# Moving two row sums and a transposing DMA in a fused attention and SwiGLU kernel

## The chip, the cores and the metric

The kernel runs on one core of a Trainium2 chip. The metric is the device time of one execution in microseconds: the median of three runs of the kernel before is 557.85 us (557.7 to 557.88). A profile is one further execution, with every instruction recorded. Engines: TensorE (PE) multiplies matrices into PSUM banks, VectorE (DVE), ScalarE (ACT) and GpSimd (POOL) work on tiles, SyncE (SP) issues DMAs. Each engine takes its instructions strictly in the order in which the program gives them, and waits on semaphores where one depends on another engine.

## The reference

Two stages follow each other. First an attention with projected keys and values (8 batches, 8 heads, 1024 tokens, head dimension 64, 64 projected keys):

```python
k_proj = np.einsum('ks,bhsd->bhkd', E, k)
v_proj = np.einsum('ks,bhsd->bhkd', F, v)
scores = scale * np.matmul(q, k_proj.transpose(0, 1, 3, 2))
attn = np.exp(scores - np.max(scores, axis=-1, keepdims=True))
attn = attn / (np.sum(attn, axis=-1, keepdims=True) + 1e-09)
attn_out = np.matmul(attn, v_proj)
```

Then a gated feed-forward block over the 8192 tokens of 512 features, with 1536 hidden features:

```python
g = x @ w_gate
silu = g * (1.0 / (1.0 + np.exp(-g)))
out = (silu * (x @ w_val)) @ w_out
```

Inputs and output are float32 in HBM.

## The kernel before

**Chunks and iterations.** The feed-forward work is cut into 16 chunks of 512 tokens, two per batch, and each chunk into 12 iterations f, one per 128 hidden features. The main loop (L986 to L995) runs over these 192 iterations. In each, f_g (L534) multiplies four gate matmuls into a gps bank, ScalarE takes the Silu, f_v (L544) multiplies four value matmuls into a vps bank, and VectorE multiplies the two into hT (L550). There are two gps and two vps banks.

**The output product.** w_out is applied with a seven-product scheme of quarter blocks: h_sum (L600) adds or subtracts quarters of hT, w_sum does so for w_out, and f_m (L676) runs the products of the chunk *before*, in 14 steps: seven (n = 0 to 6) for the first half of the tokens, seven for the second, each of six matmuls (m_mm, L624). After some steps come combinations: m_34 (L648; a ScalarE copy and a GpSimd add) after n = 1, m_52 (L655) after n = 3, m_16 (L660; a VectorE add at L663, then a GpSimd subtraction at L664) after n = 5, m_7 (L666; a VectorE add at L669 and the output DMA on SP) after n = 6. The seventh product, n = 6, is accumulated into the bank that m_16's add has read, so it follows that add. Step n runs at f = (0, 1, 2, 3, 4, 4, 5) for the first half and (6, 7, 8, 9, 10, 10, 11) for the second (L981). The sums for m = 1, 6 and 7 are each one wide VectorE instruction at the ends of f = 1, 2, 3 of the next chunk (L980); those for m = 5 and 2 go to GpSimd in small pieces at f = 6 to 11 (L972).

**Slots.** While the chunks of batch b - 1 run, the attention of batch b is prepared. Its steps are written into a table of slots by hand (put, L732; place, L735). An iteration t has two slots: 2t between f_g and f_v, and 2t + 1 behind f_v and behind all late work of the iteration (h_sum and f_m). A batch b has a stretch of 48 slots beginning at s0 = 48 (b - 1): slots 0 to 23 lie in the first chunk of the stretch (A below), 24 to 47 in the second (B). All slot numbers below are relative to s0. So in chunk B, slot 26 is before hT of f = 1, slot 28 before hT of f = 2, 30 before hT of f = 3; slot 33 is behind m_16 of the first half, slot 35 behind its m_7.

**The steps of attention.** A batch has eight score units j of 128 by 512 scores. For each, u_S (L357) multiplies q by the projected keys and ScalarE takes the exponential into a tile ee; u_R (L393) takes row sums and reciprocals on VectorE (L397, L398); u_N (L401) normalises on GpSimd (L412) into a tile AAd and calls u_Z (L426), which adds the row sums into a check sum zsum on GpSimd (L428). Units 0 to 3 belong to the first half of the batch's tokens, 4 to 7 to the second. When four units are normalised, u_AD (L349) issues a transposing DMA on SP, from AAd into a tile AT. u_PVt multiplies AT by the projected values much later: for the second half at slot 56. There are four ee tiles, two AAd tiles and two AT tiles.

**Other entries of the slots.** u_TD (L341) issues the transposing DMA of q on SP: for the next batch at slots 42 and 44. The loads of k, v and two q halves of the batch after are issued by GpSimd at slots 24, 26, 28 and 30 of the stretch (batch 2's stretch: 28, 30, 32 and 34; batch 7's has none); within a slot loads go first (L960). In batch 7's stretch slot 38 also holds u_sum (L772), which reduces zsum on VectorE, and slot 40 a small matmul that reads its result.

Before the change the units of the second group have their scores at slots 25, 25, 27, 27, their row sums and normalisations at 26, 27, 30, 31, and their transposing DMA at 36.

Of the kernel before, what the change touches and what calls it, by code (L numbers as in the profile page):

```python
# [42 lines left out]
def kernel(  # L43
# [688 lines left out]
    def put(s, fn, *a):  # L732
        slots[s].append((fn, a))

    def place(b):  # L735
        s0 = 48 * (b - 1)
        if b == 1:
            put(22, u_TD, 1, 0)
            put(29, u_K1, 1)
            put(32, u_KT, 1)  # L740
            put(40, u_V1, 1)
            sa = (35, 36, 37, 38, 41, 42, 43, 44)
            put(41, u_AD, 1, 0)
            put(30, u_TD, 1, 1)
            put(47, u_AD, 1, 1)
            put(46, u_PVt, 1, 0, (0, 1), ("aa", "av"))
        else:
            if b == 2:
                put(s0 + 10, u_KV, b)
            else:  # L750
                put(s0 + 8, u_KV, b, "kv", (0, H), "v")
            put(s0 + (13 if b == 2 else 11), u_KT, b)
            put(s0 + (9 if b == 2 else -6), u_TD, b, 0)
            put(s0 + (11 if b == 2 else -4), u_TD, b, 1)
            sa = [s0 + j for j in ((15, 15, 17, 17) if b == 2 else (13, 13, 15, 15)) + (25, 25, 27, 27)]
            put(s0 + 25, u_AD, b, 0)
            put(s0 + 36, u_AD, b, 1)
            put(s0 + 44, u_PVt, b, 0, (0, 1), ("aa", "yz"))
        for j in range(NJ):
            put(sa[j], u_S, b, j)  # L760
            at = sa[j] + (1 if b == 1 else 1 + j % 4)
            put(at, u_R, b, j)
            put(at, u_N, b, j)
        put(s0 + (68 if b == 1 else 56), u_PVt, b, 1, (0, 1), ("aa", "yz"))
# [52 lines left out]
    with tc.manual_schedule():  # L817
# [132 lines left out]
        for b in range(1, B):  # L950
            place(b)
        for b in range(2, B):
            s0 = 48 * (b - 1) - (20 if b == 3 else 24)
            at = (43, 43, 44, 45) if b == 2 else (s0, s0 + 2, s0 + 4, s0 + 6)
# [75 lines left out]
```

## Time and profile before

| what | us |
|---|---|
| median of 3 runs | 557.85 |
| the profiled execution, time | 558.25 |
| the profiled execution, span from first to last instruction | 556.6 |
| TensorE busy | 538.9 |
| VectorE busy | 323.7 |
| GpSimd busy | 308.0 |
| ScalarE busy | 262.1 |

The time of the profiled execution lies 1.65 us over its span. Busy time is the sum over an engine's instructions, averaged over the whole run; it doesn't tell what one stretch is bound by. A row of the timeline reads: start in us, duration in us, engine, line, operation, output<-input, shapes, count, and in square brackets the idle time of the engine before it with what ended that. Where several matmuls are merged, the duration is that of the group; the ends of matmuls are modelled, so the distance of two starts is the safer measure. A row of the list of waits reads: engine, waiting line, what it waited for, total us, times, longest.

### The profile page before, as it was taken

To read this page: it belongs to the slowest core of one execution; us is meant where nothing else is said; L and a number is where in the kernel's file an instruction comes from. 1 tells how busy PE (TensorE), PEld (TensorE's weight loads), DVE (VectorE), ACT (ScalarE), POOL (GpSimd) and SP (SyncE) were. 2 spreads that over 40 slices of the span, in tenths; PEclk is the share of its full clock that TensorE was granted. 3 is DMA by queue.
4 is the path that set the end of the run, shared out by engine and by line. 5 is a ranking of instruction groups with operands and counts; after the bars stand their busy time and mean duration, and the time that the engine had idled before them with its cause. 6 is when DMAs were issued, how large, how long until landed. Compare 5 with 4: busy or idle time off the path is not lost. (4 is left out here: it accounts for less than half of the span.)

```text
span 556.6 us, 9399 instructions
## 1 busy us (share of the span) xinstructions
PE 538.9 (97%) x3558; PEld 314.2 (56%) x3558; DVE 323.7 (58%) x546; ACT 262.1 (47%) x441; POOL 308.0 (55%) x428
## 2 busy tenths in 40 slices
PE   7999999998999989999999989999899999999996
PEld 4654545565556655556455555566555665555565
DVE  3787884667356654568346483465835666343553
ACT  3565453672446624556336544465344652442321
POOL 6862494468517764197532974248660666425162
PEclk9999999999999999999999999999999999999999
DMA  9999969728941894109910299114990023010003
GB/s 200 189 197 190 181 134 182 159 75 127 205 86 39 161 217 114 39 1 208 234 51 38 61 181 214 39 39 87 199 179 30 38 77 77 38 39 38 7 33 118
DMA packets 112226, 62.92 MB, mean 113 GB/s; under 512 B 65968, under 2 KB 103856, under 8 KB 112176
## 3 DMA queue, kind: packets, MB, share of 16 engines
q0 software_dynamic: 43952, 29.49, 37.2%
q1 hardware_dynamic: 67392, 31.46, 23.3%
q10 hardware_dynamic: 832, 1.31, 0.8%
q8 instruction: 29, 0.48, 0.3%
q14 instruction: 21, 0.17, 0.1%
HBM read 60.29 MB, written 16.78 MB: 138 GB/s over the span
## 5 line engine op out<-in xcount | busy, mean ns | idle before, releaser
L525 PE MATMUL vps<-xT,wv 128*128 128x512 bf16 (+1 forms) x776 | 197.6, 377 | 0.9 <-DMA wv<-in_moe_w_val_dram 0.9
L525 PE MATMUL gps<-xT,wg 128*128 128x512 bf16 (+1 forms) x772 | 196.5, 377 | 0.0
L550 DVE TENSOR_TENSOR hT<-th,vps 128x512 bf16<-128x512 f32 x156 | 106.3, 682 | 143.6 <-PE vps L525 130.1
L541 ACT ACTIVATE th<-gps 128x512 f32<-128x512 f32 x156 | 93.2, 597 | 185.1 <-PE gps L525 180.6
L617 POOL TENSOR_TENSOR hs<-hT 128x256 bf16<-128x256 bf16 x180 | 118.4, 683 | 50.4 <-DVE hT L550 47.9
L525 PEld LDWEIGHTS <-wv 128*128 128x128 bf16 x776 | 74.1, 98 | 91.0 <-issue 6.5
L634 PEld LDWEIGHTS <-hs 128*128 128x128 bf16 x900 | 88.0, 98 | 43.7 <-issue 9.6
L525 PEld LDWEIGHTS <-wg 128*128 128x128 bf16 x776 | 74.1, 98 | 51.4 <-issue 0.2
L664 POOL TENSOR_TENSOR tt<-tt,ysb 128x512 f32<-128x512 f32 x28 | 35.5, 1268 | 89.6 <-DVE tt L663 89.5
L412 POOL TENSOR_TENSOR AAd<-ee,zr 128x512 bf16<-128x512 f32 x56 | 58.5, 1044 | 47.8 <-ACT ee L375 17.6
L634 PE MATMUL yps<-ws,hs 128*128 128x256 bf16 x540 | 68.6, 273 | 8.2 <-DVE tt L663 8.1
L617 DVE TENSOR_TENSOR hs<-hT 128x1536 bf16<-128x1536 bf16 (+1 forms) x49 | 57.9, 1187 | 0.1
L397 DVE TENSOR_REDUCE zr<-ee 128x8 f32<-128x512 f32 x64 | 43.3, 677 | 20.5 <-ACT ee L375 20.2
L634 PE MATMUL yps<-ws,hT 128*128 128x256 bf16 x360 | 48.8, 273 | 0.0
L634 PE MATMUL yps<-wo,hs 128*128 128x256 bf16 x360 | 48.6, 273 | 0.1
L653 POOL TENSOR_TENSOR tt<-xs 128x256 f32<-128x256 f32 x30 | 22.8, 761 | 40.3 <-ACT xs L651 40.3
L634 PEld LDWEIGHTS <-hT 128*128 128x128 bf16 x360 | 35.2, 98 | 16.0
L375 ACT ACTIVATE ee<-sc 128x512 f32<-128x512 f32 x64 | 35.7, 606 | 4.3 <-PE sc L367 2.9
L658 ACT COPY ysb<-yps 128x512 f32<-128x512 f32 x30 | 17.6, 586 | 27.3 <-PE yps L634 27.3
L651 ACT COPY xs<-yps 128x512 f32<-128x512 f32 x30 | 17.7, 590 | 25.1 <-PE yps L634 25.0
L480 ACT CAST xT<-pv 128x512 bf16<-128x512 f32 x56 | 28.7, 599 | 0.0
L538 ACT ACTIVATE th<-gps 128x512 f32<-128x512 f32 x35 | 20.9, 598 | 16.5 <-PE gps L525 16.5
(112 smaller groups left out, 407.9 us busy)
## 6 DMA issues: line engine op xcount, KB each, us to landing
out_dram<-ysb SPq DMA_DIRECT2D x27, 512.0 KB, 2.9
qb<-in_q_dram POOLq DMA_DIRECT2D x14, 512.0 KB, 13.1
kb<-in_k_dram POOLq DMA_DIRECT2D x7, 1024.0 KB, 10.9
vb<-in_v_dram POOLq DMA_DIRECT2D x7, 1024.0 KB, 15.2
wo<-in_moe_w_out_dram POOLq DMA_DIRECT2D x2, 768.0 KB, 21.8
out_dram<-ysb SPq DMA_DIRECT2D x6, 256.0 KB, 2.4
kraw<-in_k_dram ACTq DMA_DIRECT2D x2, 512.0 KB, 4.9
qb<-in_q_dram POOLq DMA_DIRECT2D x4, 256.0 KB, 7.9
```

The lines of the kernel that those rows point to most:

```text
L375: nc.scalar.activation(out=e[:].rearrange("p h j k -> p (h j k)"), in_=ps[:].rearrange("p a k -> p (a k)"), func=AF.Exp, scale=scale,)
L397: nc.vector.reduce_sum(out=z, in_=e[:], axis=AX.X)
L412: eng.tensor_tensor(out=a.rearrange("p j h k -> p h j k"), in0=ee.pop((b, u))[:], in1=r.unsqueeze(3).to_broadcast([P, 4, 2, KP]), op=ALU.mult,
L480: nc.scalar.copy(out=xT[b, ch][:, kt, :], in_=ps[:])
L525: nc.tensor.matmul(out=ps[:, ts], lhsT=(wg, wv)[w][:, kt, f * P : (f + 1) * P], rhs=x[:, kt, ts], start=(kt == 0), stop=(kt == NKT - 1),)
L538: nc.scalar.activation(out=th[:], in_=ps[:], func=AF.Tanh, scale=0.5)
L541: nc.scalar.activation(out=th[:], in_=ps[:], func=AF.Silu)
L550: nc.vector.tensor_tensor(out=hT[c][:, f, :], in0=th[:], in1=ps[:], op=ALU.mult)
L617: eng.tensor_tensor(out=hs[c, m][:, fs, :], in0=quarter(hT[c], *a)[:, fs], in1=quarter(hT[c], *b)[:, fs], op=op,)
L634: nc.tensor.matmul(out=ps, lhsT=lhsT, rhs=ws[m][:, f, :] if rhs is None else rhs, start=(start and f == 0), stop=(f == HF - 1), skip_group ...
L653: nc.gpsimd.tensor_tensor(out=t[:, 0], in0=xs[:, 0], in1=xs[:, 1], op=ALU.add)
L664: nc.gpsimd.tensor_tensor(out=t[:], in0=t[:], in1=yo[c, p][:, 1:3], op=ALU.subtract)
```

## The change

For batches 2 to 7 the row sums and the normalisations (with their additions to zsum) of units 4 to 7 are put at slots 26, 28, 33 and 35 instead of 26, 27, 30 and 31. The transposing DMA of the second group is put at slot 38 instead of 36. Units 0 to 3 stay at their slots (the expression for them is the former one), and so does all of batch 1.

```diff
             put(s0 + 25, u_AD, b, 0)
-            put(s0 + 36, u_AD, b, 1)
+            put(s0 + 38, u_AD, b, 1)
             put(s0 + 44, u_PVt, b, 0, (0, 1), ("aa", "yz"))
         for j in range(NJ):
             put(sa[j], u_S, b, j)
-            at = sa[j] + (1 if b == 1 else 1 + j % 4)
+            at = sa[j] + 1 if b == 1 else sa[j] + 1 + j % 4 if j < 4 else s0 + (26, 28, 33, 35)[j - 4]
             put(at, u_R, b, j)
             put(at, u_N, b, j)
```

## The prediction

> **What bounds the kernel now.** I read three views in turn: the page for the engine that is always busy, the list of waits for what ever stops it, and the timeline around one stop. Unit names as in the section on the kernel: sum1, sum6, sum7 are the three whole-width h_sum calls on VectorE (L617), q0 and q1 the two q loads that GpSimd issues, A and B the two chunks of a batch's stretch.
>
> ```profile
> PE 538.9 (97%) x3558; PEld 314.2 (56%) x3558; DVE 323.7 (58%) x546; ACT 262.1 (47%) x441; POOL 308.0 (55%) x428
> L634 PE MATMUL yps<-ws,hs 128*128 128x256 bf16 x540 | 68.6, 273 | 8.2 <-DVE tt L663 8.1
> PE yps L634 <- DVE tt L663: 8.1, 6, 1.5
> ```
>
> TensorE is busy 538.9 of 556.6 us. Of its few waits one stands out: product 7 waits for the add of m_16 (L663), 8.1 us in six waits. Taken window by window, it falls once in the stretch of each of batches 2 to 7: five of 1.5 us and, for batch 7, one of 0.6. They sit always at f = 5 of chunk B, where product 7 of the first half (f_m n = 6) overwrites the bank that m_16 must have read. The fifth of them on VectorE, GpSimd and TensorE:
>
> ```profile
> 391.58 1.04 POOL L412 TENSOR_TENSOR AAd<-ee,zr 128x512 bf16<-128x512 f32 x1 [1.73 <-DVE zr L398]
> 391.99 1.45 DVE L617 TENSOR_TENSOR hs<-hT 128x1536 bf16<-128x1536 bf16 x1
> 393.36 0.67 DVE L397 TENSOR_REDUCE zr<-ee 128x8 f32<-128x512 f32 x1
> 393.47 1.81 POOL L129 DMA_DIRECT2D qb<-in_q_dram  x2
> 394.19 0.65 DVE L550 TENSOR_TENSOR hT<-th,vps 128x512 bf16<-128x512 f32 x1
> 394.76 2.42 DVE L617 TENSOR_TENSOR hs<-hT 128x1536 bf16<-128x1536 bf16 x1
> 395.29 1.06 POOL L412 TENSOR_TENSOR AAd<-ee,zr 128x512 bf16<-128x512 f32 x1
> 395.57 1.03 PE L525 MATMUL gps<-xT,wg 128*128 128x512 bf16 x4
> 396.44 1.03 PE L525 MATMUL vps<-xT,wv 128*128 128x512 bf16 x4
> 397.10 0.67 DVE L397 TENSOR_REDUCE zr<-ee 128x8 f32<-128x512 f32 x1
> 397.93 0.65 DVE L550 TENSOR_TENSOR hT<-th,vps 128x512 bf16<-128x512 f32 x1
> 398.49 0.41 DVE L663 TENSOR_TENSOR tt<-tt,yps 128x256 f32<-128x256 f32 x1
> 398.96 0.81 PE L634 MATMUL yps<-ws,hs 128*128 128x256 bf16 x6 [1.50 <-DVE tt L663]
> 399.61 1.03 PE L525 MATMUL gps<-xT,wg 128*128 128x512 bf16 x4
> ```
>
> The DVE rows follow without a gap: sum6, row sum of unit 6, hT3, sum7, row sum of unit 7, hT4, m_16. TensorE has finished the vps matmuls at 397.30 (396.44 and four times 0.215; the listed 1.03 contains a modelled tail) and m_16 only ends at 398.90.
>
> What the stop costs is best taken from the starts of the gate matmuls. An iteration of four gps, four vps and six yps takes 2.38 us everywhere undisturbed. With the stop it takes 399.61 - 395.57 = 4.04. The five stops read 4.03 or 4.04, that of batch 7 reads 3.14. So they cost 5 x 1.65 + 0.76 = **9.0 us**, where the wait list, which counts from modelled ends, says 8.1. Between 113 and 545 us all other iterations over 2.38 us have extra matmuls in them and no wait listed.
>
> **The change part by part**, over batches 2 to 7.
>
> **VectorE.** Nothing is added or removed. The row sum of unit 5 goes from slot 27 to 28, between sum1 and hT2 as before: no move in VectorE's queue. Unit 6 goes from between sum6 and hT3 to just behind m_16; unit 7 from between sum7 and hT4 to just behind m_7. One row sum with its reciprocal takes 394.19 - 393.36 = 0.83 us of queue, so m_16 loses 2 x 0.83 = 1.66 us of work ahead of it.
>
> The lengths of sum6 and sum7 change too. Undisturbed sums of this form are listed at 0.95 (chunk A of the next batch). Here sum6 is issued while GpSimd's normalisation of unit 5 runs (391.58 to 392.62), ends at 393.44, 0.82 after it, and sum7 (2.42) spans the end of the loads and the whole normalisation of unit 6 (to 396.35), ending 0.83 behind it. So sums and GpSimd's work exclude each other. With unit 6 normalised at slot 33, what can hold sum7 is q1's issue alone: GpSimd is free of zsum at 393.47, as before, q1 takes half of 1.81, to 394.38. Then: sum6 to 393.36, hT3 0.57 to 393.93, sum7 held until 394.38 and 0.82 long to 395.20, hT4 0.56 to 395.76, m_16 0.41 to about 396.2. TensorE wants it at 397.30: **1.1 us to spare**, the wait is gone in whole. Stop shorter than full removal would need m_16 later than 397.3.
>
> **GpSimd's queue.** Unit 5's normalisation and zsum add go behind the load that sits in slot 28: q0 in batches 3 to 6, the k load in batch 2, none in batch 7. So that load is issued directly behind m_34's add, which ends at 389.86, while sum1 (issued 389.26) wants to start. The trace doesn't show that neighbourhood. From below it costs nothing, as sum6 was served ahead of the zsum add queued behind unit 5 (zsum's 0.94 instead of 0.22 shows who waited). From above it costs a whole issue, 0.91 (half of 1.81), as in sum7's row, where a load issue held the sum. A gain isn't on offer beyond the wait, which is capped by TensorE. I take nothing, since sum6's row has the same order of queueing, a compute instruction in front and a sum already waiting. Even with 0.91, m_16 ends at 397.1, still ahead of 397.3.
>
> The Trainium skill (SBUF — State Buffer, Who interferes with whom) says a tensor_tensor with both inputs in SBUF contends with GpSimd instructions that read SBUF, and, as an inference, not with descriptor generation. The row of 2.42 us speaks against the second half: q1's issue was running when sum7 began, and a sum that could run beside it would have been done by 395.6. By the rule sum7 would not be held by q1 and the spare time would be 1.5 us; the predicted time would be the same.
>
> Batch 2 has loads in slots 28, 30, 32 and 34. There v and the first q issue come back to back, now without unit 6 between them. In its own stretch zsum ends at 127.1, two issues of 0.9 run to 128.9, sum7 ends at 129.7, m_16 at 130.7; TensorE is ready at 130.02 + 0.86 = 130.9. 0.2 to spare, and up to 0.75 of wait left if its k issue (0.94) also beats sum1. I take none of that.
>
> Units 6 and 7 go behind m_16's subtraction (L664, 1.27). That subtraction used to wait behind unit 7's normalisation and start at 399.34; now it starts as soon as m_16 ends. Each unit adds 1.04 + 0.22 = 1.26 just ahead of the h_sum calls of f = 6. Those start when hT6 is there, about 3.4 us after m_16; unit 7 would end some 0.5 us after that. GpSimd recovers it: from f = 6 to 11 it has 9.8 us of work in 17.0. Cost nothing.
>
> **Behind m_16 on VectorE.** Row sum 6 is now ahead of hT5, row sum 7 ahead of hT6. This order is in the trace: batch 1 has a row sum just behind m_16 at its own chunk.
>
> ```profile
> 113.59 0.42 DVE L663 TENSOR_TENSOR tt<-tt,yps 128x256 f32<-128x256 f32 x1 [0.62 <-PE yps L634]
> 113.93 0.68 DVE L397 TENSOR_REDUCE zr<-ee 128x8 f32<-128x512 f32 x1
> 115.31 0.69 DVE L550 TENSOR_TENSOR hT<-th,vps 128x512 bf16<-128x512 f32 x1 [0.47 <-PE vps L525]
> 115.96 0.69 DVE L669 TENSOR_TENSOR ysb<-tt,yps 128x512 f32<-128x512 f32 x1
> 117.70 0.69 DVE L550 TENSOR_TENSOR hT<-th,vps 128x512 bf16<-128x512 f32 x1 [1.05 <-PE vps L525]
> ```
>
> hT still waits 0.47 us for TensorE after the row sum, and that iteration takes 2.38 us. Behind m_7 VectorE stands idle 1.05, in which row sum 7's 0.83 fits. Without that cover hT6 would come under 1 us late; the vps bank has a twin, so TensorE wouldn't ask for it for another 2.4.
>
> **The transposing DMA on SP** goes from slot 36 to 38. Between them SP has no other entry (m_7's store is in 35, the next batch's q transpose in 42). It is issued at 401.88 now; with 1.65 us less before it that is 400.2, and unit 7's new normalisation would release it at about 400.7, 0.5 later. It lands in 7.8 (16.0 at most); its reader, the pv matmuls of slot 56, run at 425.77. Nothing. In batch 7 the reduce over zsum (slot 38) waits for unit 7's zsum add; its reader on TensorE is at slot 40 and has some 2 us left.
>
> **The sum.** The profiled execution took 558.25 us (span 556.6); without 9.0 it is 549.25 (span 547.6). The median of the runs, 557.85, lies 0.4 below the profiled one; from it 548.85. I say 548.9.
>
> **The rivals.**
> 1. *Part of the wait stays.* GpSimd's loads win the port twice where I let them win once or not at all, so that m_16 is 2 x 0.94 = 1.9 us later than worked out. Then 0.8 us is left in each of batches 3 to 6, the full 1.65 in batch 2, none in batch 7: 4.9 of the 9.0 stays, 553.8. For it: the 2.42 us row. Against it: sum6 was served in front of a queued instruction.
> 2. *Another wait takes its place.* Row sum 6 holds hT5, so TensorE waits for a vps bank instead of m_16. That needs hT5 over 2.4 us late. Then about 557.9. Against it: batch 1's rows.
> 3. *Slower.* The transposing DMA, released by unit 7 and issued into the busiest stretch (GpSimd's loads are landing there), comes too late for the pv matmuls, which then stop TensorE. It lands at 401.88 + 7.8 = 409.7, which leaves 16 us to 425.77. It is a loss only from there on: with 2 us beyond it in each of six batches, 12 lost against 9.0 gained, 560.9. Against it: even the longest landing, 16.0, ends at 417.9.
>
> **How the numbers follow.** Whole removal 0.76 (548.2 to 549.8, the spread of the runs and 0.75 for batch 2 on it); part stays 0.15 (549.8 to 553.8); replaced 0.04; slower 0.05. The bound for a difference is 0.2%, 1.1 us. Faster: 0.76 + 0.15 and a little of the second rival, 0.92; same 0.03; slower 0.05. The range begins at 548.2, since no other wait is left to gain from, and reaches half way into the partial case, 552.0.
>
> **What would show it.** Right: no wait of TensorE for L663, iterations of 2.38 us at f = 5 of chunk B in all six stretches, sum7 at about 1.3 us or less, DVE rows in the order sum7, hT4, m_16, row sum, hT5, m_7, row sum. Wrong: sum1 at over 2 us, an iteration over 2.5 us at f = 5 or 6, a wait for hT, or pv matmuls that wait for a DMA. Most likely to break the figure is who gets the port when a load issue and a sum meet.

## The result and the profile after

The changed kernel takes 548.94 us in the median (548.71 to 548.98) against 557.87 for the kernel before (four runs each): a ratio of 0.984, with a 95% interval of 0.9822 to 0.9857. That is 8.93 us less, where the prediction had 9.0 less and 548.9. The profiled execution took 548.71 us with a span of 547.2, 9.4 less than the span before.

The list of what TensorE waited for, after, in full. A row reads: engine, waiting line, what it waited for, total us, times, longest.

```profile
PE warm L856 <- DVE zeros L834: 1.4, 1, 1.4
PE vps L525 <- DMA wv<-in_moe_w_val_dram: 0.9, 1, 0.9
PE sc L367 <- DVE BD L164: 0.7, 1, 0.7
PE efp L844 <- DMA Fraw<-in_F_dram: 0.3, 1, 0.3
PE pv L488 <- ACT BDV L257: 0.2, 1, 0.2
PE yps L634 <- DVE ysb L703: 0.2, 1, 0.2
```

The row for L663, 8.1 us in six waits, is gone and none has taken its place: five of these rows belong to the start of the kernel, the last to its end. The iteration at f = 5 of chunk B takes 2.38 us in all six stretches, as an undisturbed one does.

The timeline of VectorE after, in the stretch that answers to the one shown of before (hT2 to hT6; the short rows of the reciprocals are left out):

```profile
384.62 0.65 DVE L550 TENSOR_TENSOR hT<-th,vps 128x512 bf16<-128x512 f32 x1
385.19 1.46 DVE L617 TENSOR_TENSOR hs<-hT 128x1536 bf16<-128x1536 bf16 x1
386.57 0.68 DVE L550 TENSOR_TENSOR hT<-th,vps 128x512 bf16<-128x512 f32 x1
387.17 0.94 DVE L617 TENSOR_TENSOR hs<-hT 128x1536 bf16<-128x1536 bf16 x1
388.04 0.67 DVE L550 TENSOR_TENSOR hT<-th,vps 128x512 bf16<-128x512 f32 x1
389.04 0.42 DVE L663 TENSOR_TENSOR tt<-tt,yps 128x256 f32<-128x256 f32 x1 [0.33 <-PE yps L634]
389.38 0.68 DVE L397 TENSOR_REDUCE zr<-ee 128x8 f32<-128x512 f32 x1
390.76 0.69 DVE L550 TENSOR_TENSOR hT<-th,vps 128x512 bf16<-128x512 f32 x1 [0.47 <-PE vps L525]
391.40 0.69 DVE L669 TENSOR_TENSOR ysb<-tt,yps 128x512 f32<-128x512 f32 x1
392.01 0.68 DVE L397 TENSOR_REDUCE zr<-ee 128x8 f32<-128x512 f32 x1
393.14 0.69 DVE L550 TENSOR_TENSOR hT<-th,vps 128x512 bf16<-128x512 f32 x1 [0.22 <-PE vps L525]
```

Two things left the way of m_16 (L663): the two row sums, now behind it and behind m_7, and 1.48 us of sum7, which takes 0.94 us where it took 2.42. VectorE now reaches m_16 early and waits 0.33 us for TensorE's own product. Both hT behind the moved row sums still wait for TensorE.

GpSimd after, around sum7 (387.17):

```profile
382.33 0.72 POOL L653 TENSOR_TENSOR tt<-xs 128x256 f32<-128x256 f32 x1
383.00 0.94 POOL L129 DMA_DIRECT2D qb<-in_q_dram  x1
384.80 1.03 POOL L412 TENSOR_TENSOR AAd<-ee,zr 128x512 bf16<-128x512 f32 x1 [0.86 <-DVE zr L398]
385.80 0.93 POOL L428 TENSOR_TENSOR zsum<-zsum,zr 128x16 f32<-128x16 f32 x1
386.67 0.94 POOL L129 DMA_DIRECT2D qb<-in_q_dram  x1
389.62 1.26 POOL L664 TENSOR_TENSOR tt<-tt,ysb 128x512 f32<-128x512 f32 x1 [2.00 <-DVE tt L663]
```

Sum7 runs from 387.17 to 388.11 while q1's load is being issued, 386.67 to 387.61, and isn't held by it. And q0's issue at 383.00, now directly behind m_34's addition, doesn't lengthen sum1: 1.42 us, 1.41 before.

And TensorE there, gate matmuls of f = 5, its value matmuls, product 7 and the next gate matmuls:

```profile
388.77 1.03 PE L525 MATMUL gps<-xT,wg 128*128 128x512 bf16 x4
389.63 1.03 PE L525 MATMUL vps<-xT,wv 128*128 128x512 bf16 x4
390.49 0.82 PE L634 MATMUL yps<-ws,hs 128*128 128x256 bf16 x6
391.15 1.03 PE L525 MATMUL gps<-xT,wg 128*128 128x512 bf16 x4
```

Product 7 starts at 390.49, straight behind the value matmuls. m_16 ended at 389.46, so there are 1.03 us to spare, and 1.36 on VectorE with the 0.33 it idles.

### The profile page after: what moved, and what is told of

Read it like the earlier page. It is cut to its first block, busy times and chain, and to the rows that moved or that the text cites. A ratio compares the mean times of both kernels' runs of the same rounds, so it can differ in the third digit from the quotient of the medians.

```text
span 547.2 us, 9325 instructions
## 1 busy us (share of the span) xinstructions
PE 534.7 (98%) x3496; PEld 314.1 (57%) x3558; DVE 317.3 (58%) x546; ACT 262.2 (48%) x441; POOL 303.7 (56%) x428
## 4 chain that ended last, share of the span: by engine, by line
PE 94%; DMA 2%; POOL 1%; issue 1%; ACT 0%; DVE 0%; POOLq 0%; DVEq 0%; ACTq 0%
PE vps L525 30%; PE gps L525 29%; PE yps L634 25%; PE sc L367 3%; DMA wv<-in_moe_w_val_dram 2%; PE kvp L176 2%; PE yps L568 2%; PE pv L471 1%; POOL vb L120 0%; POOL qb L129 0%; POOL AA L412 0%; PE kvp L215 0%; PE kvp L200 0%; PE qTp L332 0%; PE pv L451 0%
## 5 line engine op out<-in xcount | busy, mean ns | idle before, releaser
L525 PE MATMUL vps<-xT,wv 128*128 128x512 bf16 (+1 forms) x755 | 195.4, 377 | 2.0 <-DMA wv<-in_moe_w_val_dram 0.9
L525 PE MATMUL gps<-xT,wg 128*128 128x512 bf16 (+1 forms) x733 | 193.0, 377 | 1.7
L617 DVE TENSOR_TENSOR hs<-hT 128x1536 bf16<-128x1536 bf16 (+1 forms) x49 | 50.0, 1026 | 0.1
```

The costliest lines, as they stand in the source:

```text
L525: nc.tensor.matmul(out=ps[:, ts], lhsT=(wg, wv)[w][:, kt, f * P : (f + 1) * P], rhs=x[:, kt, ts], start=(kt == 0), stop=(kt == NKT - 1),)
L617: eng.tensor_tensor(out=hs[c, m][:, fs, :], in0=quarter(hT[c], *a)[:, fs], in1=quarter(hT[c], *b)[:, fs], op=op,)
```

## The experiments

The theory: TensorE stopped because m_16 came late on VectorE, by two causes, the row sums ahead of it and the hold of sum7. Rivals: the later transposing DMA brings the gain; VectorE's load as such, rather than one wait, binds the stretch; and, on the hold, that it comes from the loads. In each result the time after "against" is that of the kernel before, run beside it; the ratio is followed by its 95% interval.

### One unit at a time

Unit 7 alone, as an edit of the kernel after:

```diff
-            at = sa[j] + 1 if b == 1 else sa[j] + 1 + j % 4 if j < 4 else s0 + (26, 28, 33, 35)[j - 4]
+            at = sa[j] + 1 if b == 1 else sa[j] + 1 + j % 4 if j < 4 else s0 + (26, 27, 30, 35)[j - 4]
```

> Only unit 7 moves (row sum and normalisation at slot 35), units 5 and 6 stay at 27 and 30, the transposing DMA at 38. If m_16 is late by what lies ahead of it on VectorE, it gains one row sum, 0.83 us, in each of batches 2 to 6 and 0.76 in batch 7: 5 x 0.83 + 0.76 = 4.9 us, 553.0, and the iteration at f = 5 of chunk B stays at about 3.2 us. Sum7 keeps its 2.42 us. If the later transposing DMA is what gains, 548.9.

Measured: 553.22 us against 558.21, ratio 0.9912 (0.9895 to 0.9928), 5.0 us less. TensorE still waits for L663, and sum7 keeps its 2.42 us (1.52 in batch 7):

```profile
PE yps L634 <- DVE tt L663: 3.5, 5, 0.7
```

Unit 6 alone:

```diff
-            at = sa[j] + 1 if b == 1 else sa[j] + 1 + j % 4 if j < 4 else s0 + (26, 28, 33, 35)[j - 4]
+            at = sa[j] + 1 if b == 1 else sa[j] + 1 + j % 4 if j < 4 else s0 + (26, 27, 33, 31)[j - 4]
```

> Only unit 6 moves (slot 33), units 5 and 7 stay at 27 and 31, the transposing DMA at 38. Under the theory that sum7 is held by unit 6's normalisation as well, m_16 gains the row sum, 0.83 us, and the hold of sum7, 2.42 - 0.94 = 1.48: 2.3 us, more than the 1.65 of the stop, so the whole 9.0 us, 548.9. If a row sum counts only by its place in VectorE's queue, as much as unit 7 alone: 4.9 us, 553.0.

Measured: 549.48 us against 558.21, ratio 0.9842 (0.9826 to 0.9859), 8.7 us less, the same as the whole change within the interval. Sum7 takes 0.95 and no wait for L663 is left.

```profile
387.49 0.95 DVE L617 TENSOR_TENSOR hs<-hT 128x1536 bf16<-128x1536 bf16 x1
```

So the two moves aren't of equal worth: unit 7's is worth its 0.83 us of queue, unit 6's that and the hold. Unit 6 alone does it; with it moved, unit 7 can stay ahead of m_16, since 2.3 us are freed and 1.65 were needed.

### The transposing DMA alone, and the change without it

```diff
-            put(s0 + 36, u_AD, b, 1)
+            put(s0 + 38, u_AD, b, 1)
```

> The kernel before with the transposing DMA alone at slot 38. By the theory of VectorE's queue no change, 557.9, since SP has nothing between the slots. By the rival that the transposing DMA collided with something in its old slot, up to the whole gain, 548.9.

Measured: 558.21 us against 558.21, ratio 1.0002 (0.9992 to 1.0011). The reverse, the kernel after with this DMA back at slot 36:

> The kernel after with the transposing DMA back at slot 36. SP has nothing between slots 36 and 38, so no change: 548.9. If its later place carries part of the gain, slower than that by over 1 us.

Measured: 548.85 us against 558.17, ratio 0.9834 (0.9816 to 0.9852). The DMA's slot carries nothing: on SP nothing stands between 36 and 38, and what releases it is the same in either slot. In the kernel before it follows m_7's store by 0.49 us (401.88 and 401.39; 402.29 and 401.81 from slot 38). In the kernel after it is issued 0.03 after unit 7's normalisation has ended (394.08; 393.01 + 1.04), and from slot 36 as well (394.22; 393.15 + 1.04). That rival is out.

### Normalisations moved, row sums left

```diff
+            an = at if b == 1 or j < 6 else s0 + (33, 35)[j - 6]
             put(at, u_R, b, j)
-            put(at, u_N, b, j)
+            put(an, u_N, b, j)
```

> Row sums stay where they were before (26, 27, 30, 31), only the normalisations of units 6 and 7 go to slots 33 and 35 on GpSimd; the transposing DMA is at 38. VectorE's order is that of before. If unit 6's normalisation is what holds sum7, sum7 takes 0.94 instead of 2.42 (1.52 in batch 7) and m_16 is 1.48 (0.58) us earlier: 5 x 1.48 + 0.58 = 8.0 us, 549.9. If the load issue holds it, as the prediction had it, sum7 still waits for the end of the loads, m_16 gains 1.05 in each of batches 2 to 6: 5.8 us, 552.0. If the row sums on VectorE are all that counts, 557.9.

Measured: 550.01 us against 558.21, ratio 0.9851 (0.9835 to 0.9868), 8.2 us less. VectorE (some rows left out) and GpSimd around sum7:

```profile
387.61 0.67 DVE L397 TENSOR_REDUCE zr<-ee 128x8 f32<-128x512 f32 x1
388.44 0.65 DVE L550 TENSOR_TENSOR hT<-th,vps 128x512 bf16<-128x512 f32 x1
389.01 0.95 DVE L617 TENSOR_TENSOR hs<-hT 128x1536 bf16<-128x1536 bf16 x1
389.87 0.68 DVE L397 TENSOR_REDUCE zr<-ee 128x8 f32<-128x512 f32 x1
391.27 0.41 DVE L663 TENSOR_TENSOR tt<-tt,yps 128x256 f32<-128x256 f32 x1
```

```profile
387.72 1.81 POOL L129 DMA_DIRECT2D qb<-in_q_dram  x2
391.83 1.26 POOL L664 TENSOR_TENSOR tt<-tt,ysb 128x512 f32<-128x512 f32 x1 [2.30 <-DVE tt L663]
```

The order on VectorE is that of before and the two load issues lie over sum7 as before; only the normalisation behind them is missing. Sum7 falls from 2.42 to 0.95. So most of the gain, 8.2 of 8.9 us, can be had without moving any VectorE instruction. The rest is a stop that the wait list, which counts from modelled ends, does not show: the iteration at f = 5 of chunk B takes 2.57 us by the starts, 0.19 too much, six times. The run also contradicts the prediction's reading of the row: the load issues alone don't hold sum7, unit 6's normalisation is needed for it.

### Work put back ahead of m_16

Two and four more row sums of unit 6, their results unused, at slot 32, between sum7 and hT4:

```diff
+    def u_X(b, u):
+        for i in range(2):    # 4 in the second kernel
+            nc.vector.reduce_sum(
+                out=xtra[:, i].rearrange("p (h j) -> p h j", j=2), in_=ee[b, u][:], axis=AX.X
+            )
...
+            put(s0 + 32, u_X, b, 6)
```

> The kernel after with two more row sums of unit 6 (results unused) at slot 32 of batches 2 to 7, so between sum7 and hT4 on VectorE. In the profile after, VectorE is idle 0.33 us ahead of m_16 and m_16 ends 1.03 us before TensorE wants it, 1.36 to spare. Two row sums without reciprocal take about 2 x 0.61 = 1.2 us: no change, 548.9 (at most 0.5 us more in all, if one takes 0.72). If the kernel is bound by VectorE's busy time in this stretch rather than by this one wait, 6 x 1.2 = 7 us more, 556.

Measured: 549.30 us against 558.17, ratio 0.9835 (0.9818 to 0.9851): 0.45 us above the kernel without them (548.85, the one with the DMA at slot 36, timed beside it), inside the intervals. VectorE has 7 us more to do, and it costs nothing that can be told.

> The same with four more row sums, 4 x 0.61 = 2.44 us, 1.1 beyond what there is to spare: TensorE stops again for m_16 in each of six batches, 6 x 1.1 = 6.6 us more, 555.5 (up to 557.5 if one takes 0.72). If the spare time isn't a threshold but VectorE's load counts evenly, twice what the two cost.

Measured: 555.23 us against 558.17, ratio 0.9941 (0.9924 to 0.9958), 5.9 us above two row sums and 6.4 above none. The waits of TensorE, the four row sums, and the stop in TensorE's timeline:

```profile
PE yps L641 <- DVE tt L670: 4.8, 6, 0.8
393.00 2.45 DVE L404 TENSOR_REDUCE xtra<-ee 128x8 f32<-128x512 f32 x4
395.38 0.67 DVE L557 TENSOR_TENSOR hT<-th,vps 128x512 bf16<-128x512 f32 x1
```

```profile
393.73 1.03 PE L532 MATMUL gps<-xT,wg 128*128 128x512 bf16 x4
396.43 0.81 PE L641 MATMUL yps<-ws,hs 128*128 128x256 bf16 x6 [0.81 <-DVE tt L670]
397.08 1.03 PE L532 MATMUL gps<-xT,wg 128*128 128x512 bf16 x4
```

(The lines are shifted by the added function: L670 is m_16's addition, L404 the added row sums.) The four take 395.38 - 393.00 = 2.38 us of VectorE's queue, 1.02 more than the 1.36 to spare that were read from the profile after. An iteration takes 397.08 - 393.73 = 3.35, so 0.97 too much, and 6 x 0.97 = 5.8 is about what the time shows (5.9 above two row sums). So the first two row sums cost nothing, and of the next two only what goes beyond the spare time: a threshold.

### Loads away from the normalisation

The kernel before, the q loads of batches 4 to 7 at slots 32 and 34:

```diff
-            at = (43, 43, 44, 45) if b == 2 else (s0, s0 + 2, s0 + 4, s0 + 6)
+            at = (43, 43, 44, 45) if b == 2 else (s0, s0 + 2, s0 + 8, s0 + 10) if b > 3 else (s0, s0 + 2, s0 + 4, s0 + 6)
```

> The kernel before with the two q loads of batches 4 to 7 issued at slots 32 and 34 instead of 28 and 30 of the stretch before, so none just ahead of unit 6's normalisation in the stretches of batches 3 to 6. If the loads make the difference between a stop of 1.65 us (batches 2 to 6) and one of 0.76 (batch 7, without loads), sum7 falls from 2.42 to 1.5 us and the stop to about 0.75 in four stretches: 4 x 0.9 = 3.6 us, 554.3. If the hold of sum7 has nothing to do with the loads, 557.9.

Measured: 554.58 us against 558.17, ratio 0.993 (0.9913 to 0.9946), 3.6 us less. Sum7 takes 1.52 in the four stretches and TensorE's wait falls to batch 7's value in them.

```profile
392.09 1.04 POOL L412 TENSOR_TENSOR AAd<-ee,zr 128x512 bf16<-128x512 f32 x1 [0.90 <-DVE zr L398]
392.43 1.52 DVE L617 TENSOR_TENSOR hs<-hT 128x1536 bf16<-128x1536 bf16 x1
```

The normalisation starts 0.15 us after unit 6's reciprocal has ended (391.94), where it started 1.02 after it in the kernel before (395.29 against 394.27), and sum7 ends 0.82 or 0.83 after the normalisation in both. So between these two kernels the loads matter by what they do to the normalisation: they delay its start, and with it the end of the hold. That this isn't the whole of it is what the next runs show.

### What precisely keeps the sum out

In the kernel before, sum7 was issued 0.5 us before the normalisation started by the profile, and yet ran after it. Three kernels were to show why. First the v load and both q loads together at slot 30, just ahead of the normalisation:

```diff
-            at = (43, 43, 44, 45) if b == 2 else (s0, s0 + 2, s0 + 4, s0 + 6)
+            at = (43, 43, 44, 45) if b == 2 else (s0, s0 + 6, s0 + 6, s0 + 6) if b > 3 else (s0, s0 + 2, s0 + 4, s0 + 6)
```

> The kernel before with the v load and both q loads of batches 4 to 7 issued together at slot 30, directly ahead of unit 6's normalisation, in the stretches of batches 3 to 6. Sum7 is issued when the loads have about 1.3 us to go, the normalisation is ready but queued behind them. If whichever of the two starts first goes first, sum7 runs beside the loads in 0.94 us, the stop shrinks by 1.48 in four stretches, 5.9 us, 552.0. If an instruction that is ready and queued behind a load already keeps the sum out, sum7 waits for the last load and the whole normalisation, about 3.3 us, and the stop grows by one load issue, 0.9 in four stretches, 3.5 us, 561.4.

Measured: 554.44 us against 558.36, ratio 0.9931 (0.9914 to 0.9947). Neither: sum7 takes 1.52 in four stretches.

```profile
392.22 1.52 DVE L617 TENSOR_TENSOR hs<-hT 128x1536 bf16<-128x1536 bf16 x1
```

```profile
390.94 0.94 POOL L120 DMA_DIRECT2D vb<-in_v_dram  x1
391.87 1.76 POOL L129 DMA_DIRECT2D qb<-in_q_dram  x2
393.62 1.08 POOL L412 TENSOR_TENSOR AAd<-ee,zr 128x512 bf16<-128x512 f32 x1
```

It ends at 393.74, only 0.12 us after the normalisation's recorded start at 393.62. If it needs the 0.82 us here too that it took behind the end of a hold elsewhere, it was let in at about 392.92 (an estimate), 0.7 before that start and while the last load was being issued. The Trainium skill (Perfetto Trace Analysis, DMA Instruction — SWDGE (GPSIMD)) says that descriptors are made by two of GpSimd's processors; from that came the reading that the others begin the normalisation early, which no run here shows directly. The numbers fitted, so it was set against a simpler reading by shifting the loads, in this kernel with three loads, with two small additions on GpSimd:

```diff
+    def u_pad(n):
+        for _ in range(n):
+            nc.gpsimd.tensor_tensor(out=xtra[:], in0=xtra[:], in1=xtra[:], op=ALU.add)
...
+            if b > 2:
+                put(s0 + 29, u_pad, 2)
```

> The kernel with three loads, and two additions of 16 columns on GpSimd (results unused) ahead of the loads in batches 3 to 7, which shift the loads by about 0.36 us. In the run with three loads sum7 was held 0.6 us, until neither the last load's end nor the normalisation's. Two explanations. (a) GpSimd's work is spread over several cores, only some of them write descriptors, and the others begin unit 6's normalisation as soon as its reciprocal is there: in the run with three loads 391.74 + 0.14 + 1.04 = 392.92, and 0.82 more for sum7 is 393.74, as recorded. Then shifting the loads changes nothing for sum7: 1.52 us, the time as with three loads, 554.4. (b) Sum7 gets in at the border between two load issues. Then it starts 0.36 us later and takes 1.85 to 1.9, and the stop grows by 0.36 in four stretches, 555.9; or it gets in at the border before, 0.95 to 1.1 us, and the stop all but goes, 552.

Measured: 552.24 us against 557.95, ratio 0.99 (0.9883 to 0.9916). Sum7 isn't held at all, 0.95 (L622 is h_sum, L121 the v load):

```profile
390.26 0.95 DVE L622 TENSOR_TENSOR hs<-hT 128x1536 bf16<-128x1536 bf16 x1
389.76 0.94 POOL L121 DMA_DIRECT2D vb<-in_v_dram  x1 [0.27 <-issue]
```

The additions shifted the loads against sum7 by 0.78 us (it was issued 1.28 after the v load's start, now 0.50), not by 0.36. Reading (a) falls as it stood, and so does the first half of (b), since sum7 began in the middle of the v load's issue. The second half of (b) has the time right, 552, but not the reason: sum7 waited for no border. A third reading, with a limit on how far ahead the early start can reach, was put to the same additions in front of the loads of the kernel before (they sit behind unit 5 at slot 27):

> The kernel before, loads where they were, with the two small additions of 16 columns on GpSimd between unit 5's zsum addition and the q loads in batches 3 to 7; in the run before they shifted the loads by 0.77 us. A third explanation fits all runs so far: GpSimd's cores that write no descriptors begin unit 6's normalisation while a load is running, but only when at most one further load stands between. It predicts: they start it 0.14 after its reciprocal, are done 1.04 later, sum7 then runs 0.82, and the loads now end late enough that the remaining cores don't take the port before it. Sum7 takes 1.52 us instead of 2.42 in batches 3 to 6, the stop falls from 1.65 to about 0.75: 3.6 us, 554.3. If the normalisation as a whole, as it stands in the profile, must end first, sum7 takes 2.42 + 0.77 = 3.2 us and the kernel 4 x 0.77 = 3.1 us more than before, 561. If sum7 gets in at the border between the two loads, 1.3 us, 553.4; if it runs at once, 0.95, 552.

Measured: 552.39 us against 558.31, ratio 0.9894 (0.9878 to 0.9911), 5.9 us less, the case "if it runs at once". Again sum7 isn't held (L398 and L399 are the row sum and its reciprocal, L417 the normalisation, L404 the additions):

```profile
389.84 0.20 DVE L399 RECIPROCAL zr<-zr 128x8 f32<-128x8 f32 x1
390.52 0.95 DVE L622 TENSOR_TENSOR hs<-hT 128x1536 bf16<-128x1536 bf16 x1
391.39 0.68 DVE L398 TENSOR_REDUCE zr<-ee 128x8 f32<-128x512 f32 x1
```

```profile
389.25 0.50 POOL L404 TENSOR_TENSOR xtra<-xtra 128x16 f32<-128x16 f32 x2
390.01 1.81 POOL L130 DMA_DIRECT2D qb<-in_q_dram  x2 [0.26 <-issue]
391.84 1.06 POOL L417 TENSOR_TENSOR AAd<-ee,zr 128x512 bf16<-128x512 f32 x1
```

The third reading falls too. With the additions the first load starts after a gap of 0.26 us marked as issue, and together with the end of unit 6's reciprocal (390.01 and 389.84 + 0.20 = 390.04); in the kernel before it started 0.8 us ahead of that end (393.47 and 394.07 + 0.20 = 394.27). Whether one of these decides isn't shown by any run. **Open**: what lets a normalisation that stands behind load issues keep a VectorE sum out before its own recorded start, in some placements and not in others. Shown is that it does so in the kernel before, that sum7 is 1.48 us longer by it in each of five stretches, and that the hold is gone when the normalisation isn't there.

## Why the prediction was right

**The place and the size of the stop.** It rested on the wait of product 7 for m_16, sized by the starts of the gate matmuls: 9.0 us. Measured 8.93. The wait list alone, 8.1, would have been 0.8 short; the starts are the better measure, as each stop is 1.65 by them and 1.50 by the list.

**The row sums on VectorE**, 0.83 us each: unit 7 alone gave 5.0 where 5 x 0.83 + 0.76 = 4.9 was worked out.

**The hold of sum7 was mis-attributed.** The prediction let q1's load issue hold sum7 until 394.38 and kept, for its row, a full issue of 0.91 as the upper bound on sum1. The runs show a sum beside a load issue at 0.94 or 0.95 us and sum1 unchanged. The hold needs unit 6's normalisation; in the kernel before it stands behind two loads, and why that holds a sum before the normalisation's own start is open, as said above. So sum7 was 0.4 us dearer in the prediction than it is (1.27 of queue instead of 388.04 - 387.17 = 0.87), and the 1.1 us to spare agree with the measured 1.03 only because m_16 now meets another limit, TensorE's own product, that the working left out: luck. For batch 2 the prediction let sum7 wait for two load issues and left 0.2 us; there too sum7 took 0.94 beside them (from 127.36), and m_16 ended 1.04 ahead of product 7 (129.65 and 130.69). The time was safe from this, since the stop can't become less than nothing. The Trainium skill's rule (SBUF — State Buffer, Who interferes with whom), against which the prediction set its reading of the row, agrees with what was measured here: a two-input sum at 0.94 us during q1's issue.

**GpSimd's queue and SP.** The subtraction of m_16 starts 0.16 us after m_16's addition has ended (389.62, 389.04 + 0.42). The h_sum calls of f = 6 start at 394.19, 0.36 after hT6 has ended, and lose nothing further on: the next group starts 6.96 us after product 7 as before (397.45 - 390.49, 405.92 - 398.96). That 0.36 comes close to the 0.5 of the prediction is luck too:

```profile
393.01 1.04 POOL L412 TENSOR_TENSOR AAd<-ee,zr 128x512 bf16<-128x512 f32 x1 [0.95 <-DVE zr L398]
```

hT6 ends 4.4 us after m_16 (393.83 and 389.46), where the prediction took 3.4 from rows in which m_16 was late, and unit 7's normalisation waits 0.95 us for its own row sum, which the working left out. The transposing DMA is issued 3.59 us after product 7 starts (394.08 - 390.49) where it was 2.92, 0.67 later instead of the 0.5 estimated; its reader doesn't wait.

**Behind m_16.** Batch 1's rows as a model for row sum 6 ahead of hT5 held to the digit: hT waits 0.47 in both.

**The rivals.** A part of the wait staying was refuted by the rows of sum1 and sum7; a new wait for a vps bank by the hT rows; the transposing DMA by moving it alone in both directions, and its late landing by the list of waits, in which no pv matmul waits for a DMA.

## What to carry to other kernels

Where an engine takes its instructions in the program's order, a wait of the bottleneck is paid by whatever stands ahead of the awaited instruction; look at that chain row by row, and move what nobody awaits behind it, even to a place where the engine seems as busy. Size a stop of TensorE by the distance of starts to an undisturbed iteration. And a long row beside another engine's work says that there is a collision, not with what: undo one neighbour at a time before blaming one.

## What the runs showed of the hardware

A VectorE addition or subtraction of two bf16 tiles in SBUF (128 x 1536) takes 0.94 to 0.95 us undisturbed, also while GpSimd issues a load, but 1.40 to 1.52 when a GpSimd multiplication or addition on SBUF tiles is running when it starts. With the normalisation queued behind two load issues it took 2.42, behind three 1.52, and 0.95 in both cases with two small additions ahead of the loads. A small GpSimd addition (16 columns, 0.22 us) takes 0.93 to 0.96 when it has to wait for such a sum.

Not expected: two useless additions of 16 columns on GpSimd in five stretches make the kernel before 5.9 us faster, 552.39 against 558.31, by freeing sum7 in four of them (4 x 1.48 = 5.9). So a shift of the load issues by 0.78 us against sum7 was worth 1% of this kernel.
